# Turned scores in a top-k attention kernel: products of k and q in place of transpositions

## The chip, the cores and the metric

The kernel runs on one core of one Trainium2 chip. A core has a matrix engine (TensorE, PE in the profile; its weight loads are PEld), a vector engine (VectorE, DVE), a scalar engine (ScalarE, ACT), GpSimd (POOL) and a queue engine for transfers (SyncE, SP). The metric is the device time of one execution in microseconds. The kernel before takes 929.28 us, the median of three runs (928.62 to 929.35).

## The reference

Eight batches of eight heads, 576 positions, 64 numbers a head, all fp32. First attention that keeps the 32 highest scores of each row, then a mixture-of-depths layer on the result.

```python
scores = scale * np.matmul(q, k.transpose(0, 1, 3, 2))
kth = np.partition(scores, -top_k, axis=-1)[..., -top_k:-top_k + 1]
scores = np.where(scores >= kth, scores, -1000000000.0)
attn = np.exp(scores - np.max(scores, axis=-1, keepdims=True))
attn = attn / (np.sum(attn, axis=-1, keepdims=True) + 1e-09)
x = np.matmul(attn, v)                    # then (B, H, S, D) -> (B, S, H*D)

scores = np.einsum('bsd,d->bs', x, w_gate)
for b in range(B):                        # the 128 positions with the highest gate
    top_idx = np.argpartition(-scores[b], capacity)[:capacity]
    xe = x[b, top_idx]
    ye = np.maximum(xe @ w1, 0.0) @ w2
    g = 1.0 / (1.0 + np.exp(-scores[b, top_idx]))
    out[b, top_idx] = x[b, top_idx] + g[:, None] * ye
```

The expert's hidden width is 1024.

## The kernel before

**Units.** The work is cut into units of two heads by up to 128 rows of q. A batch has four row tiles of 128 rows with four units each (t = 0 to 3, "whole units") and a last row tile of 64 rows (t = J = 4) with two units, in which four heads are stacked two by two on the 128 partitions ("stacked units"): 18 units a batch, 144 in all.

**The pipeline.** A loop over n (lines 758 to 862) works on several units at once, and every engine executes its instructions in the order written there:

- unit n+1: `multiply` makes the scores, rows of q on the partitions, as k and q products in PSUM (`ps`); `keep` copies them to SBUF as `sc` on ScalarE.
- unit n: `find_bound` on VectorE takes the highest 8 of each of 8 pieces of a row and narrows them to the 24th highest of these candidates.
- unit n-1: two sign passes (`part`) on ScalarE count and mark what lies above that bound, and GpSimd multiplies scores and signs into `y`.
- unit n-2: `find_kth` on VectorE finds the 32nd highest from `y`.
- unit n-3: `mask` makes `less` (bf16), larger than zero where a score is below the 32nd: ScalarE for the first head, GpSimd for the second.
- unit n-4: the scores are needed turned, with keys on the partitions, for the product with v. `turn_last` and `turn` transpose `sc` on TensorE, nine tiles of 128x128, and behind each transposition a second matmul adds `less` times `out_of_reach` (a diagonal of -2^90) into the same PSUM, so that masked scores vanish in the exponential. ScalarE takes exponentials from PSUM (`last`, then `pT` for each head) and `values` multiplies them by v on TensorE.

In one turn of the loop TensorE's order is: turning of unit n-4, scores of unit n+1, values of unit n-4, then a step of the mixture of the batch before (expert products `h_ps`, `y_ps`) or of the load of the next batch, as `mix_at` and `load_at` (lines 728 and 737) set them. ScalarE's is: exponentials of n-4, copies put off by `late` (flushed at line 786), the mask of n-3, the score copies of n+1, the sign passes of n-1, the copies of the values.

**The buffers.** kT and qT of a batch hold k and q with the 64 numbers of a head on the partitions, heads of even number on partitions 0 to 63 and of odd number on 64 to 127; there are two such pairs, taken in turn by the batches. `load_kq` fetches rows, transposes them on TensorE, and copies them in. Keys 0 to 511 stand in kT at R to S (R = 64, S = 576); the last 64 stand at 0 to R and again behind. PSUM's `ps` is one buffer: the turning of the tail (`tr_last`) uses 128 columns of it that the scores of unit n+1 leave free. The score products of two heads stand on the two 64-row halves of the array. `general`, at the end, is a path for data that the fast one can't treat; the run does not enter it.

Of the kernel before, what the change touches and what calls it, by code (L numbers as in the profile page):

```python
# [11 lines left out]
FP32 = mybir.dt.float32  # L12
# [18 lines left out]
J = 4  # L31
# [14 lines left out]
def kernel(  # L46
# [12 lines left out]
    P = nc.NUM_PARTITIONS  # L59
    B, H, S, D = q.shape  # L60
# [4 lines left out]
    JP = J * P  # L65
    R = S - JP
# [22 lines left out]
    ps_tr = ctx.enter_context(tc.tile_pool(name="ps_tr", bufs=2, space=PS))  # L89
# [4 lines left out]
    ident = const.tile([P, P], FP32, name="ident")  # L94
# [24 lines left out]
    out_of_reach = const.tile([P, P], BF16, name="out_of_reach")  # L119
# [25 lines left out]
    vbufs = []  # L145
# [13 lines left out]
    def load_weights():  # L159
# [6 lines left out]
    pe, dve, act, pool, sp = (  # L166
        InOrder(tc, e)
        for e in (nc.tensor, nc.vector, nc.scalar, nc.gpsimd, nc.sync)
    )
# [13 lines left out]
        flush()  # L183


    def room_for_qkv(b):

        kT = kqpool.tile([P, NHP, R + S], FP32, name="kT")
        qT = kqpool.tile([P, NHP, S], FP32, name="qT")
        return kT, qT, vbufs[b % 2]

    def load_kq(kb, qb, kT, qT, issue=None):

        last = [ldpool.tile([R, H, D], FP32, name=f"last{i}", bufs=1) for i in range(2)]

        def fetch_last(w, dma):
            src = (kb, qb)[w]
            dma.dma_start(
                out=last[w], in_=src[:, JP:S, :].rearrange("h p d -> p h d")
            )

        def fetch(i, dma=sp):
            hp, src = i // 2, (kb, qb)[i % 2]
            rows = ldpool.tile([P, J, 2, D], FP32, name="rows")
            for hh in range(2):  # L210
                dma.dma_start(
                    out=rows[:, :, hh, :],
                    in_=src[2 * hp + hh, 0:JP, :].rearrange("(p j) d -> p j d", j=J),
                )
            return rows

        issue = issue or sp
        fetch_last(0, sp)
        fetch_last(1, issue)
        fetched = [fetch(0), fetch(1, issue), fetch(2)]  # L220
        yield
        tr = ps_misc.tile([P, 512], FP32, name="tr", tag="misc")
        for i in range(2 * NHP):
            w, hp = divmod(i, NHP)
            pe.transpose(
                tr[:, i * R : (i + 1) * R],
                last[w][:, 2 * hp : 2 * hp + 2, :].rearrange("p h d -> p (h d)"),
                ident[0:R, 0:R],
            )

        def keep_last(tails=tr.rearrange("p (w c r) -> p w c r", w=2, c=NHP)):
            act.copy(out=kT[:, :, 0:R], in_=tails[:, 0, :, :])
            act.copy(out=kT[:, :, S : S + R], in_=tails[:, 0, :, :])
            act.mul(out=qT[:, :, JP:S], in_=tails[:, 1, :, :], mul=SMALLER)

        late.append(keep_last)
        yield
        for i in range(2 * NHP):
            tr = ps_misc.tile([P, 512], FP32, name="tr", tag="misc")
            for c in range(J):  # L240
                pe.transpose(
                    tr[:, c * P : (c + 1) * P],
                    fetched[i][:, c, :, :].rearrange("p h d -> p (h d)"),
                    ident,
                )

            def keep_rows(i=i, tr=tr):
                if i % 2 == 0:
                    act.copy(out=kT[:, i // 2, R:S], in_=tr)
                else:  # L250
                    act.mul(out=qT[:, i // 2, 0:JP], in_=tr, mul=SMALLER)

            late.append(keep_rows)
            if i + 3 < 2 * NHP:
                fetched.append(fetch(i + 3))
            yield

    def load_v(vb, vs):
        vt, vpair = vs
        v_rows = vb[:, JP:S, :].rearrange("h p d -> p h d")  # L260
        for hh in range(2):
            sp.dma_start(
                out=vpair[hh * R : (hh + 1) * R, :, hh, 0:D], in_=v_rows[:, hh::2, :]
            )
        for h in range(H):
            sp.dma_start(
                out=vt[:, h, :, 0:D],
                in_=vb[h, 0:JP, :].rearrange("(p j) d -> p j d", j=J),
            )
# [5 lines left out]
    def heads_of(t, g):  # L275

        if t == J:
            return [[(4 * g + i, 0), (4 * g + 2 + i, R)] for i in range(2)]
        return [[(2 * g + i, 0)] for i in range(2)]
# [107 lines left out]
                )  # L391
        return less

    def turn_some(tr, z, less):

        pe.transpose(tr, z, ident)
        if less is not None:
            pe.matmul(
                tr, less, out_of_reach, start=False, stop=True, skip_group_check=True
            )  # L400

    def turn(i, z, less=None):

        tr = ps_tr.tile([P, 512], FP32, name="ptr")
        for c in range(J):
            at = slice(c * P + i * R, (c + 1) * P + i * R)
            turn_some(
                tr[:, c * P : (c + 1) * P],
                z[:, i, at],
                None if less is None else less[:, i, at],  # L410
            )
        return tr

    def turn_last(z, ps, less=None):

        tr = ps[:, 1, 1, 512 - P : 512]
        last = [  # L420
            a and a.rearrange("p i s -> p (i s)")[:, JP : JP + P] for a in (z, less)
        ]
        turn_some(tr, *last)
        return tr

    def values(t, g, pT, last, av, vs):
# [296 lines left out]
    units = [(b, t, g) for b in range(B) for t in range(NT) for g in range(groups(t))]  # L723
# [19 lines left out]
                break  # L743
            mix_steps.setdefault(n, []).append(b)
    mixtures = {}
    qkv = {0: room_for_qkv(0)}
    first_load = load_kq(k[0], q[0], *qkv[0][0:2], issue=act)
    next(first_load)
    next(first_load)
    flush()  # L750
# [7 lines left out]
    for n in range(-1, N + 6):  # L758
# [11 lines left out]
        if is_unit(n - 4) or is_unit(n + 1):  # L770
            ps = room_for_scores()
        if is_unit(n - 4):
            sc, less = scs.pop(n - 4), masks.pop(n - 4)
            tr_last = turn_last(sc, ps, less)
            trs = [turn(i, sc, less) for i in range(2)]
            pT = ptpool.tile([P, 2, J, P], FP32, name="pT")
            last = ptpool.tile([P, P], FP32, name="last")
            act.activation(last, tr_last, AF.Exp, scale=scale)
            for i in range(2):
                act.activation(  # L780
                    pT[:, i, :, :],
                    trs[i].rearrange("p (c i) -> p c i", c=J),
                    AF.Exp,
                    scale=scale,
                )
# [55 lines left out]
        if gating is not None:  # L841
            b, t = gating
# [11 lines left out]
        if n in load_steps:  # L854
            b, begin = load_steps[n]
            if begin:
                qkv[b] = room_for_qkv(b)
                loading = load_kq(k[b], q[b], *qkv[b][0:2])
            next(loading)
        b, i = divmod(n, per_batch)  # L860
        if i == v_at and 0 <= b < B - 1:
            load_v(v[b + 1], qkv[b + 1][2])

    for b in (B - 2, B - 1):
        for _ in mixtures[b]:
# [65 lines left out]
    def general(b, row0):  # L931
        def of(a):
            return a[bass.ds(b, 1)].rearrange("o a s d -> (o a) s d")

        kT, qT, vs = room_for_qkv(0)
        for _ in load_kq(of(k), of(q), kT, qT):
            flush()
        load_v(of(v), vs)
        x = xpool.tile([P, NT, HD], FP32, name="x")
        gate = xpool.tile([P, NT], FP32, name="gate")  # L940
        for t in range(NT):
            xs = xpool.tile([P, H, DE], FP32, name="xs")
            for g in range(groups(t)):
                ps = room_for_scores()
                multiply(t, g, kT, qT, ps)
                p = general_weights(keep(ps))
                ps = room_for_scores()
                av = ps_av.tile([P, 512], FP32, name="av")
                pT = ptpool.tile([P, 2, J, P], FP32, name="pT")
                last = ptpool.tile([P, P], FP32, name="last")  # L950
                for i in range(2):
                    nc.scalar.copy(
                        out=pT[:, i, :, :],
                        in_=turn(i, p).rearrange("p (c i) -> p c i", c=J),
                    )
                nc.scalar.copy(out=last, in_=turn_last(p, ps))
                values(t, g, pT, last, av, vs)
                keep_values(t, g, av, xs)
            rows = R if t == J else P
            den = stats.tile([P, H], FP32, name="den")  # L960
            divide(rows, xs, x[0:rows, t, :], den[0:rows, :])
            dot_tile(t, x, gate)
        store(out[bass.ds(b, 1)].rearrange("o s n -> (o s) n"), x)
        rank = stats.tile([P, NT], FP32, name="rank")
        for _ in mixture(row0, gate, rank, exact=True):
            flush_both()
# [40 lines left out]
```

## Time and profile before

| | |
|---|---|
| median of three runs | 929.28 us |
| the profiled execution, own time | 923.33 us |
| its span, first to last instruction | 921.5 us |
| mean granted TensorE clock | 0.975 |
| busy share of the span: TensorE, VectorE, ScalarE, GpSimd | 88%, 90%, 84%, 79% |
| start of the first turning | 37.4 us |
| mean time of a batch (18 units), batches 1 to 6 | 104.8 us |

The page gives busy time, groups of instructions by form with their mean duration, idle time and what ended it; the timeline gives instructions by start time, runs of equal ones merged into one line with their count. TensorE's instructions are pipelined, so a mean duration is longer than the distance between two starts. Nearly all instructions are recorded at line 42, that of the helper that issues them; so groups are told by their tiles (out<-in).

### The profile page before, as it was taken

How to read it: one execution, taken by the hardware profiler on the slowest of the kernel's cores; microseconds unless marked ns; L12 is line 12 of the kernel's file. 1: busy time of each engine (PE TensorE's matmuls, PEld its weight loads, DVE VectorE, ACT ScalarE, POOL GpSimd, SP SyncE). 2: the span in 40 equal slices, each digit the busy share in tenths (PEclk: the TensorE clock that was granted, in tenths of full speed). 3: DMA queues.
4: the chain of work that ended last, by engine and by line, in shares of the span. 5: the costliest groups of instructions: out<-in, count | busy, mean ns of one | idle time of the engine just before them, and what ended most of it. 6: DMA issues, size and time to landing. Idle time of an engine off the chain costs nothing.

```text
span 921.5 us, 28585 instructions
## 1 busy us (share of the span) xinstructions
PE 808.6 (88%) x9839; PEld 617.3 (67%) x9839; DVE 832.5 (90%) x4966; ACT 772.5 (84%) x1883; POOL 732.4 (79%) x800
## 2 busy tenths in 40 slices
PE   5699889788999899998999889998999889987935
PEld 3477666566877678766777668766787667765723
DVE  4799999999999999999999999999999999998140
ACT  3699998898998899989998999989998898987310
POOL 2589998888988898888988898889888898888210
PEclk9999999999999999999999999999999999998968
DMA  5952005112140313221140313222150211000021
GB/s 102 265 116 59 14 2 124 30 36 47 65 89 7 57 34 101 53 48 47 66 89 2 59 36 99 55 48 48 47 107 2 37 53 26 3 14 13 1 74 15
DMA packets 122200, 50.40 MB, mean 55 GB/s; under 512 B 116416, under 2 KB 116416, under 8 KB 121024
## 3 DMA queue, kind: packets, MB, share of 16 engines
q1 hardware_dynamic: 118672, 43.91, 20.3%
q0 software_dynamic: 1792, 4.20, 2.6%
q8 instruction: 80, 1.31, 0.6%
q14 instruction: 72, 0.59, 0.3%
q10 hardware_dynamic: 1584, 0.39, 0.2%
HBM read 36.93 MB, written 11.55 MB: 53 GB/s over the span
## 4 chain that ended last, share of the span: by engine, by line
DVE 35%; PE 28%; ACT 20%; POOL 6%; DMA 5%; issue 4%; SPq 0%; POOLq 0%; ACTq 0%
DVE cand L42 18%; DVE next L42 8%; ACT sides L42 7%; PE ptr L42 7%; PE ps L42 6%; ACT sc L42 5%; PE av L42 5%; PE h_ps L42 5%; DVE best L42 5%; PE y_ps L42 5%; ACT pT L42 3%; POOL y L42 2%; POOL less L42 2%; DMA row_dram<-gate 2%; DVE prod L42 2%
## 5 line engine op out<-in xcount | busy, mean ns | idle before, releaser
L42 POOL TENSOR_TENSOR y<-sc,sides 128x576 f32<-128x576 f32 x288 | 367.1, 1306 | 101.7 <-ACT sides L42 101.3
L42 DVE MAX8 cand<-sc 128x8 f32<-128x72 f32 x2304 | 331.5, 217 | 16.0 <-ACT sc L42 16.0
L42 POOL TENSOR_SCALAR less<-sc,next 128x576 bf16<-128x576 f32 x144 | 256.7, 1783 | 26.9 <-DVE next L42 17.9
L42 ACT ACTIVATE sides<-sc,seen 128x576 bf16<-128x576 f32 x288 | 221.0, 768 | 4.9
L42 PE MATMUL ptr<-ident,sc 128*128 128x128 f32 x1152 | 218.2, 283 | 0.0
L42 DVE MAX8 next<-y 128x8 f32<-128x584 f32 x288 | 204.4, 751 | 6.2 <-POOL y L42 6.2
L42 PE MATMUL ptr<-out_of_reach,less 128*128 128x128 bf16 x1152 | 209.5, 222 | 0.0
L42 PE MATMUL ps<-kT,qT 64*128 64x288 f32 (+1 forms) x1280 | 187.2, 449 | 18.2 <-ACT last L42 13.1
L42 ACT ACTIVATE pT<-ptr 128x512 f32<-128x512 f32 x288 | 163.2, 597 | 32.3 <-PE ptr L42 26.7
L42 PEld LDWEIGHTS av<-v,pT 128*64 128x64 f32 x4608 | 147.2, 138 | 57.5 <-ACT pT L42 30.7
L42 ACT COPY sc<-ps 128x576 f32<-128x576 f32 x288 | 170.7, 654 | 11.9 <-PE ps L42 10.8
L42 PEld LDWEIGHTS ptr<-ident,sc 128*128 128x128 f32 x1152 | 164.9, 143 | 14.4
L42 PEld LDWEIGHTS <-less 128*128 128x128 bf16 x1296 | 134.5, 105 | 59.2 <-POOL less L42 50.2
L42 PE MATMUL av<-v,pT 128*64 128x65 f32 x4608 | 167.5, 225 | 0.3 <-ACT pT L42 0.2
L42 DVE MAX8 best<-cand 128x8 f32<-128x64 f32 x864 | 148.8, 213 | 0.0
L42 PEld LDWEIGHTS ps<-kT,qT 64*128 64x128 f32 (+1 forms) x1280 | 100.2, 184 | 65.0 <-ACT last L42 29.0
L42 ACT ACTIVATE less<-sc,next 128x576 bf16<-128x576 f32 x144 | 113.2, 786 | 10.2 <-DVE next L42 9.8
L42 DVE MATCH_REPLACE8 cand<-best,cand 128x64 f32<-128x64 f32 x576 | 116.1, 209 | 0.0
L42 PE MATMUL ps<-out_of_reach,less 128*128 128x128 bf16 x144 | 32.2, 224 | 42.0 <-POOL less L42 42.0
L42 PE MATMUL av<-vpair,last 128*128 128x130 f32 (+1 forms) x320 | 69.0, 316 | 0.0
L42 PE MATMUL h_ps<-xeT,w 128*128 128x128 f32 x512 | 63.8, 282 | 3.8 <-ACT xeT L42 2.0
L42 PEld LDWEIGHTS h_ps<-xeT,w 128*128 128x128 f32 x512 | 60.6, 196 | 6.0 <-ACT xeT L42 2.7
(80 smaller groups left out, 842.5 us busy)
## 6 DMA issues: line engine op xcount, KB each, us to landing
rows<-in_k_dram SPq DMA_DIRECT2D x64, 128.0 KB, 3.0
v<-in_v_dram SPq DMA_DIRECT2D x64, 128.0 KB, 3.5
out_dram<-x SPq DMA_DIRECT2D x8, 1024.0 KB, 4.6
rows<-in_q_dram SPq DMA_DIRECT2D x62, 128.0 KB, 3.2
w<-in_moe_w_dram SPq DMA_DIRECT2D x2, 2048.0 KB, 13.3
gate_row<-row_dram SPq DMA_DIRECT2D x7, 288.0 KB, 4.3
last<-in_k_dram SPq DMA_DIRECT2D x8, 128.0 KB, 4.5
vpair<-in_v_dram SPq DMA_DIRECT2D x16, 64.0 KB, 3.4
```

The source lines that it names most:

```text
L42: return lambda *a, **kw: self._tc.keep_in_program_order(fn(*a, **kw))
```

## The change

The turned scores are no longer transposed from `sc` but made by a second set of products, with kT as the weights and qT streaming, for the two heads on the two 64-row halves of the array: nine tiles as before, and the mask is added behind as before. The products of the tail and of the first 128 keys stand ahead of the first mask product, then the products of the other keys, then eight mask products. Since kT and qT of a batch are now read until its last unit is turned (five turns of the loop longer), the room for the next batch's is taken only when the first copy into it is made. `turn` and `turn_last` lose their mask and serve only `general`.

```diff
+    qkv = {}
     def room_for_qkv(b):
...
-        return kT, qT, vbufs[b % 2]
-    def load_kq(kb, qb, kT, qT, issue=None):
+        qkv[b] = kT, qT, vbufs[b % 2]
+        return qkv[b]
+    def load_kq(kb, qb, room, issue=None):
+        kept = []
...
         def keep_last(tails=tr.rearrange("p (w c r) -> p w c r", w=2, c=NHP)):
+            kept.extend(room()[0:2])
+            kT, qT = kept
             act.copy(out=kT[:, :, 0:R], in_=tails[:, 0, :, :])
...
             def keep_rows(i=i, tr=tr):
+                kT, qT = kept
...
+    def multiply_turned(t, g, kT, qT, ps, less):
+        n = R if t == J else P
+        rows = heads_of(t, g)
+        tr_last = ps[:, 1, 1, 512 - P : 512]
+        trs = [ps_tr.tile([P, 512], FP32, name="ptr") for _ in range(2)]
+        for i in range(2):
+            d = slice(i * D, (i + 1) * D)
+            for h, r in rows[i]:
+                pe.matmul(
+                    tr_last[i * R : (i + 1) * R, r : r + n],
+                    kT[d, h // 2, 0:R],
+                    qT[d, h // 2, t * P : t * P + n],
+                    start=(r == 0),
+                    stop=False,
+                    skip_group_check=True,
+                )
+        for c in range(J):
+            for e in range(len(rows[0])):
+                for i in range(2):
+                    d = slice(i * D, (i + 1) * D)
+                    h, r = rows[i][e]
+                    pe.matmul(
+                        trs[i][:, c * P + r : c * P + r + n],
+                        kT[d, h // 2, R + c * P : R + (c + 1) * P],
+                        qT[d, h // 2, t * P : t * P + n],
+                        start=(c == 0 and r == 0),
+                        stop=False,
+                        skip_group_check=True,
+                    )
+            if c == 0:
+                put_out(tr_last, less.rearrange("p i s -> p (i s)")[:, JP : JP + P])
+        for i in range(2):
+            for c in range(J):
+                at = c * P + i * R
+                put_out(trs[i][:, c * P : (c + 1) * P], less[:, i, at : at + P])
+        return tr_last, trs
+    def put_out(tr, less):
+        pe.matmul(tr, less, out_of_reach, start=False, stop=True, skip_group_check=True)
...
         if is_unit(n - 4):
-            sc, less = scs.pop(n - 4), masks.pop(n - 4)
-            tr_last = turn_last(sc, ps, less)
-            trs = [turn(i, sc, less) for i in range(2)]
+            b, t, g = units[n - 4]
+            scs.pop(n - 4)
+            tr_last, trs = multiply_turned(t, g, *qkv[b][0:2], ps, masks.pop(n - 4))
...
             if begin:
-                qkv[b] = room_for_qkv(b)
-                loading = load_kq(k[b], q[b], *qkv[b][0:2])
+                loading = load_kq(k[b], q[b], lambda b=b: room_for_qkv(b))
             next(loading)
...
-            load_v(v[b + 1], qkv[b + 1][2])
+            load_v(v[b + 1], vbufs[(b + 1) % 2])
```

More of the change, by code (lines that the diff above doesn't have):

```diff
@@ L392, in mask @@
         return less
[L394 to L402, printed above, removed]
+    def multiply_turned(t, g, kT, qT, ps, less):
[34 more added lines that the diff above has]
+        return tr_last, trs
@@ L404, in turn @@
+    def put_out(tr, less):
+        pe.matmul(tr, less, out_of_reach, start=False, stop=True, skip_group_check=True)
+    def turn(i, z):
         tr = ps_tr.tile([P, 512], FP32, name="ptr")
         for c in range(J):
[L406 to L411, printed above, removed]
+            at = c * P + i * R
+            pe.transpose(tr[:, c * P : (c + 1) * P], z[:, i, at : at + P], ident)
@@ L412, in turn, with turn_last @@
         return tr
-    def turn_last(z, ps, less=None):
+    def turn_last(z, ps):
         tr = ps[:, 1, 1, 512 - P : 512]
[L420 to L423, printed above, removed]
+        pe.transpose(tr, z.rearrange("p i s -> p (i s)")[:, JP : JP + P], ident)
         return tr
@@ L745 @@
     mixtures = {}
-    qkv = {0: room_for_qkv(0)}
-    first_load = load_kq(k[0], q[0], *qkv[0][0:2], issue=act)
+    room_for_qkv(0)
+    first_load = load_kq(k[0], q[0], lambda: qkv[0], issue=act)
     next(first_load)
@@ L935, in general @@
         kT, qT, vs = room_for_qkv(0)
-        for _ in load_kq(of(k), of(q), kT, qT):
+        for _ in load_kq(of(k), of(q), lambda: qkv[0]):
             flush()
```

## The prediction

> **What bounds the kernel now.** I read the page's engine shares first, then busy time by stretches, then the groups by form, the timeline of TensorE, and last the waits.
>
> ```profile
> PE 808.6 (88%) x9839; PEld 617.3 (67%) x9839; DVE 832.5 (90%) x4966; ACT 772.5 (84%) x1883; POOL 732.4 (79%) x800
> ```
>
> ```profile
> 353.00:397.50 44.50, 44.13 (x527) 33.80 (x526) 44.09 (x272) 41.21 (x100) 38.60 (x43) 1.00 0.31 77
> 397.50:449.60 52.10, 46.11 (x622) 36.01 (x621) 51.89 (x306) 48.51 (x121) 45.73 (x50) 1.00 0.21 42
> ```
>
> The columns are stretch, length, then busy us of PE, PEld, DVE, ACT, POOL, the clock, and DMA. VectorE is busy 99% of both stretches; TensorE is busy 99% of the first (a batch's middle, where the expert products of the batch before are mixed in) and 89% of the second. So two engines sit at their limits at once: no gain on TensorE can shorten the middle by more than VectorE's 1%, and any lengthening of TensorE shows at once in the first stretch.
>
> The forms of TensorE's work:
>
> ```profile
> L42 PE MATMUL ptr<-ident,sc 128*128 128x128 f32 x1152 | 218.2, 283 | 0.0
> L42 PE MATMUL ptr<-out_of_reach,less 128*128 128x128 bf16 x1152 | 209.5, 222 | 0.0
> L42 PE MATMUL ps<-kT,qT 64*128 64x288 f32 x1024 | 164.4, 441 | 17.2 <-ACT last L42 12.3 <-ACT qT L42 2.7 <-ACT sc L42 1.3
> ```
>
> The counts tell most. 144 units with 8 transpositions each make 1152, one instruction each. But 128 whole units with 4 score products make 512, and the row has 1024: an fp32 product costs two instructions, a transposition one. Means overlap, so spacing has to come from start times:
>
> ```profile
> 387.24 1.24 PE L42 MATMUL ps<-kT,qT 64*128 64x288 f32 x8
> 388.41 1.16 PE L42 MATMUL av<-v,pT 128*64 128x65 f32 x32
> 389.50 0.49 PE L42 MATMUL av<-vpair,last 128*128 128x130 f32 x2
> 389.82 1.88 PE L42 MATMUL y_ps<-w,hT 128*128 128x512 f32 x4
> 391.54 0.27 PE L42 MATMUL ps<-ident,sc 128*128 128x128 f32 x1
> ```
>
> This unit began its turning at 385.62: turning 1.62 us, scores 1.17, attention values 1.09 and 0.32, expert products 1.72, and the next unit's turning starts without a gap. It is TensorE-bound. The spacings and the price of changing the array's tiling:
>
> ```profile
> 450.99 0.28 PE L42 MATMUL ptr<-ident,sc 128*128 128x128 f32 x1
> 451.11 0.22 PE L42 MATMUL ptr<-out_of_reach,less 128*128 128x128 bf16 x1
> 451.26 1.00 PE L42 MATMUL ps<-kT,qT 64*128 64x288 f32 x6
> ```
>
> ```profile
> 404.24 0.51 PE L42 MATMUL ps<-kT,qT 64*128 64x288 f32 x2 [0.32 <-ACT last L42]
> ```
>
> ```profile
> 404.59 0.65 PE L42 MATMUL ps<-kT,qT 64*128 64x288 f32 x4
> ```
>
> ```profile
> 405.07 0.41 PE L42 MATMUL ps<-kT,qT 64*128 64x288 f32 x2
> ```
>
> ```profile
> 446.85 2.94 PE L42 MATMUL h_ps<-xeT,w 128*128 128x128 f32 x24
> ```
>
> A transposition takes 0.115 to the next start, a mask product 0.057: a pair 0.171. Score instructions start two at a time on the two 64-row halves, 0.24 apart (404.59, 404.83, 405.07) for 288 columns. Full fp32 instructions of 128 columns run every 0.112 (2.94 for 24, the tail of one off). From a mask product (full array) to the first score product (halves) the distance is 0.15 instead of 0.057: 0.093 for the change of tiling. Then the first pair lasts 0.35 instead of 0.24: 0.105 of weight load that nothing covers.
>
> ```profile
> PE ps L42 <- POOL less L42: 42.0, 39, 3.6
> PEld av L42 <- ACT pT L42: 30.7, 79, 0.5
> ACT pT L42 <- PE ptr L42: 26.7, 63, 1.0
> ```
>
> Outside the dense stretch TensorE waits for the mask from GpSimd, 42 us in 39 of 144 units.
>
> **The change, part by part.** Removed per unit: 9 transpositions. Kept: 9 mask products. Added in a whole unit (128 rows; 128 units): 10 fp32 products, that is 20 instructions. 16 of them load 64x128 weights (128 keys of one head), 4 load 64x64 (the last 64 keys); each streams 128 queries. If the halves run together as the score products do, that is 10 slots. No row has this form; the nearest is the 0.112 of the expert products (same 128 columns, weights as wide), and two 64-row weight loads start together in the score products. 10 x 0.112 = 1.12, masks 9 x 0.057 = 0.51: 1.63 against 9 x 0.171 = 1.54 before. Bounds: 1.07 by scaling the score slot (0.24 x 128/288 x 10), 2.24 if the halves take turns.
>
> Added tilings: the old block keeps the full array throughout. The new one enters 64x64 tiles, goes to 64x128, to the full array for the first mask, back to 64x128, and again to the full array for eight masks: five changes more. Each costs 0.093 by the row above. The weights behind each: 0.105 into 128 fp32 columns (twice), 0.053 into 64 columns (estimated as half), 0.025 into a bf16 mask (twice; bounded by 0 and 0.105, the low end because bf16 loads of 128 columns have the shorter mean, 105 ns against 143). Sum 5 x 0.093 + 0.313 = 0.78; the ends are 0 (all hidden) and 0.99 (0.198 each). I take 0.78, from the rows of exactly such changes. The block: 1.63 + 0.78 = 2.41, so 0.87 more.
>
> The last-row-tile units (16, two a batch) stack two heads in 64-column products: 40 instructions, 20 slots. The 16 with 128-column weights are bounded below by 0.056 (half the columns) and above by 0.112; I take 0.112 as the load is as wide. 4 tail slots at 0.062 (32 attention-value instructions in 1.16, two at a time). 1.79 + 0.25 + 0.51 + 0.78 = 3.33: 1.79 more.
>
> The Trainium skill, "TensorEngine Tiling (Array Packing)", section Tiling Modes, says that changing the tiling mode, not just the tile, drains the engine; that speaks against interleaving masks with half-array products, and the 0.093 above agrees with it. It names no lost weight load; with drains alone the block would be 1.63 + 0.47 = 2.10 and the same sum as below would give some 980 instead.
>
> Where this lands. By the starts of the tail's transposition, one for each unit, batches 1 to 6 take 104.8 us on average. Of the 18 units up to 441.89, the ten from 338.40 to 397.47 (with expert products, or loads' transpositions between them) run with TensorE back to back, 59.07 us. Their nine whole and one stacked unit get 9 x 0.87 + 1.79 = 9.6 us, all on the path. The other eight (397.47 to 441.89, 44.4 us) hold TensorE waits: the turning block has mean 2.13 against its 1.54, about 10 us a batch. The added 7.9 there falls mostly into these waits, yet ScalarE's exponentials come later: the first head's masks were half done in the middle of the old block, now they end 0.23 before its close, 2.2 us after its start instead of 0.86. ScalarE covers this by its two sign passes (about 2.0 us after the score copies free PSUM), so some 0.2 to 0.3 a unit shows, and the queue behind it is the mask, then the score copies that free PSUM for the next block. I take 1 of the 0 to 2.5 us. 10.6 a batch over seven batches is 74; batch 0 (96.9 us, no expert products) 3. Start and end stay. Together 77: the profiled execution's 923.3 (span 921.5) becomes 1000, and the median 929.3 becomes 1006; I say 1004, a little under because a few of the ten units have short waits.
>
> The new wait: the first mask still waits for GpSimd, now with 4 products done and 6 products and 8 masks behind it, 1.5 us against the old 1.43. So where the mask is late nothing is won.
>
> Other edits, at nothing: kT and qT get their room in the tail copies instead of at the fetch. Those copies stand in ScalarE's order after the exponentials of the very unit that last reads the old kT, so they wait for nothing new, and the batch that needs them is 15 units off; if the cover went, one unit (5.8 us) a batch, seven times 5.8 at most, and only if it reached the scores. SP's fetches keep their places, and so do the value loads. Score buffers come free one step earlier; ScalarE's copies waited only 1.0 us for that. VectorE, ScalarE and GpSimd issue the same.
>
> **The rivals.** (a) The changes of tiling are hidden, the weights loaded ahead: the block is 1.63 and 2.55, the dense stretch gains 9 x 0.09 + 1.01 = 1.8 a batch, 13 in all: 942. For it: full-array weight loads are covered (0.112 a slot). Against: the 0.15 and 0.35 above.
> (b) The halves take turns: 1.12 more in a whole unit, 2.04 in a stacked one. TensorE's work in a batch is 18 x (1.54 + 1.17 + 1.09 + 0.32) = 74, loads 4, expert products 64 x 0.112 + 16 x 0.43 = 14, together 92 of 104.8; it becomes 92 + 17.5 + 22 = 131.5; seven batches of +28 and some 16 in the first: about 1145. Against: the score products' pairs.
> (c) Faster: the wait for the mask sets the pace, and behind it less is left: with free changes 6 x 0.112 + 0.51 = 1.18 instead of 1.43, in 39 units, 10 us: 919. It decides only if the two changes behind the first mask cost under 0.25 together (the rows say 0.32) and the dense stretch does not grow, while even free changes leave 1.63 over 1.54.
>
> **How the numbers follow.** Main case 0.66, its own range 970 to 1045; (a) 0.21, 930 to 970; (b) 0.07; (c) 0.04; no change 0.02. 0.2% is about what a measurement of this kernel can tell from none. Slower 0.94, same 0.02, faster 0.04. The range 945 to 1045 leaves out (b), (c), and the low part of (a).
>
> **What would show it.** About 3200 product instructions in place of 1296 transpositions. From the first tail product to the first score product about 2.4 us (3.3 stacked) in units without a wait; a unit with four y_ps instructions 6.8 instead of 5.92; a batch about 115 instead of 104.8. VectorE keeps 832 us busy but falls to about 84%, the wait of PE for POOL less shrinks well below 42. Wrong if products start singly, if first pairs behind a mask are no later than others, or if the dense stretch has slack that the busy time hides.

## The result, and the profile after

The changed kernel takes 991.18 us (median of 4 runs, 989.9 to 995.07) against 928.95 for the kernel before: 1.068 times as long, 95% interval 1.065 to 1.071. Its profiled execution took 991.56 us with a span of 989.7; the span of before was 921.5, so the two traces differ by 68 us, of which the medians show 62: the profiled execution of before (923.3 us) was faster than its timed runs here and beside the experiments, which, but for one slow run of 1403.9, took 924.2 to 935.5.

The first line of the page, then the same two stretches of a batch as in the prediction, moved to where they now lie:

```profile
PE 916.8 (93%) x11743; PEld 681.5 (69%) x11743; DVE 867.5 (88%) x4966; ACT 772.1 (78%) x1883; POOL 735.8 (74%) x800
```

```profile
371.90:422.40 50.50, 50.50 (x612) 36.20 (x608) 46.37 (x270) 40.55 (x99) 38.33 (x43) 1.00 0.27 64
422.40:469.10 46.70, 44.00 (x635) 33.37 (x634) 44.90 (x251) 40.89 (x98) 39.98 (x43) 1.00 0.23 47
```

TensorE is now busy all through the dense stretch (50.50 of 50.50 us), while VectorE, 99% before, has fallen to 92% there. TensorE alone sets the pace. One dense unit with four expert products, from TensorE's timeline:

```profile
407.91 0.44 PE L42 MATMUL ps<-qT,kT 64*64 64x128 f32 x4
408.28 0.49 PE L42 MATMUL ptr<-qT,kT 64*128 64x128 f32 x4
408.70 0.23 PE L42 MATMUL ps<-out_of_reach,less 128*128 128x128 bf16 x1
408.86 0.94 PE L42 MATMUL ptr<-qT,kT 64*128 64x128 f32 x12
409.73 0.62 PE L42 MATMUL ptr<-out_of_reach,less 128*128 128x128 bf16 x8
410.28 1.24 PE L42 MATMUL ps<-kT,qT 64*128 64x288 f32 x8
411.45 1.15 PE L42 MATMUL av<-v,pT 128*64 128x65 f32 x32
412.53 0.49 PE L42 MATMUL av<-vpair,last 128*128 128x130 f32 x2
412.86 1.88 PE L42 MATMUL y_ps<-w,hT 128*128 128x512 f32 x4
```

Turning goes from 407.91 to 410.28, 2.37 us instead of 1.62, and everything behind it is as long as before. The next unit begins at 414.67: 6.76 us for the unit instead of 5.92. The difference is 0.84, not 0.75, because the change of tiling in front of the block lies in the y_ps products' distance to it. Within the block the tail's second pair of products starts 0.16 after the first, the products' second pair 0.21 after theirs, later pairs 0.11 apart, and the masks 0.056.

The rows of waits:

```profile
ACT pT L42 <- PE ptr L42: 91.7, 143, 1.8
PEld av L42 <- ACT pT L42: 56.4, 141, 0.7
PE ps L42 <- POOL less L42: 14.8, 15, 2.2
```

ScalarE now waits for the turned scores in 143 of 144 units, 92 us instead of 27; TensorE's wait for GpSimd's mask has fallen from 42 us to 15.

By the start of each unit's block, the 68 us lie here: batch 0 takes 104.7 us instead of 96.9, batch 1 as long as before (106.9 and 107.0), batches 2 to 6 take 114.3 on average instead of 104.4 (+49.8 together), the last +10.6. Before the first block and behind the last nothing has moved (37.5 and 52.3 us in both). Of the +9.9 in such a batch, 7.6 are in the ten dense units (59.07 to 66.63) and 2.4 in the eight others (45.3 to 47.7).

The granted clock has a part in the last number. In the trace of before there are spells of 3.41 us in which TensorE is granted half its clock: one each in batches 1, 2, 4 and 6, none in batches 3 and 5. The changed kernel has none in batches 0 to 6. What a spell costs can be read from two units of before, the same one of batch 2 and of batch 3: both wait 1.84 us for GpSimd's mask, but only in the first does a spell follow (the third line; columns as in the prediction, the clock behind POOL):

```profile
302.65:310.76 8.11, 6.27 (x74) 4.15 (x75) 8.04 (x50) 5.89 (x15) 6.72 (x8) 0.79 0.63 99
407.44:414.11 6.67, 4.75 (x73) 3.52 (x74) 6.63 (x41) 5.56 (x14) 6.67 (x8) 1.00 0.76 119
305.56:308.97 3.41, 3.41 (x26) 1.73 (x24) 3.41 (x15) 2.34 (x4) 3.41 (x4) 0.50 0.84 148
```

That is 1.44 us more. Before's two batches at full clock take 103.5 us, 44.4 of them in the eight units; against these the changed kernel lost 7.6 in the dense ten and 3.3 in the eight, 10.8 a batch.

### The profile page after: what moved, and what is told of

It is laid out like the page before. It is cut to its first block, busy times and chain, and to the rows that moved or that the text cites. A ratio compares the mean times of both kernels' runs of the same rounds, so it can differ in the third digit from the quotient of the medians.

```text
span 989.7 us, 32393 instructions
## 1 busy us (share of the span) xinstructions
PE 916.8 (93%) x11743; PEld 681.5 (69%) x11743; DVE 867.5 (88%) x4966; ACT 772.1 (78%) x1883; POOL 735.8 (74%) x800
## 4 chain that ended last, share of the span: by engine, by line
PE 48%; DVE 33%; ACT 11%; DMA 4%; POOL 2%; issue 2%; SPq 0%; POOLq 0%; ACTq 0%
DVE cand L42 16%; PE ptr L42 16%; PE ps L42 12%; PE av L42 8%; DVE next L42 7%; PE h_ps L42 6%; PE y_ps L42 5%; DVE best L42 4%; ACT sc L42 3%; ACT pT L42 3%; DVE pick L42 2%; ACT less L42 2%; DMA row_dram<-gate 1%; DVE junk L42 1%; PE tr L42 1%
## 5 line engine op out<-in xcount | busy, mean ns | idle before, releaser
L42 POOL TENSOR_TENSOR y<-sc,sides 128x576 f32<-128x576 f32 x288 | 371.3, 1322 | 183.4 <-ACT sides L42 183.2
L42 ACT ACTIVATE pT<-ptr 128x512 f32<-128x512 f32 x288 | 156.3, 594 | 91.7 <-PE ptr L42 91.7
L42 PE MATMUL ptr<-qT,kT 64*128 64x128 f32 (+1 forms) x2560 | 220.0, 295 | 0.0
L42 PEld LDWEIGHTS ptr<-qT,kT 64*128 64x128 f32 x2560 | 166.3, 187 | 32.8 <-issue 22.1
L42 PE MATMUL ps<-kT,qT 64*128 64x288 f32 (+1 forms) x1280 | 185.1, 440 | 4.1 <-ACT qT L42 2.7
L42 PEld LDWEIGHTS <-less 128*128 128x128 bf16 x1296 | 79.1, 98 | 49.3 <-POOL less L42 17.8
L42 PE MATMUL ptr<-out_of_reach,less 128*128 128x128 bf16 x1152 | 90.1, 222 | 0.0
L42 PE MATMUL ps<-qT,kT 64*64 64x128 f32 (+1 forms) x640 | 63.3, 283 | 13.4 <-ACT sc L42 10.6
L42 ACT ACTIVATE last<-ps 128x128 f32<-128x128 f32 x144 | 39.6, 275 | 44.9 <-PE ps L42 44.7
```

The lines of the kernel that those rows point to most:

```text
L42: return lambda *a, **kw: self._tc.keep_in_program_order(fn(*a, **kw))
```

## Experiments

The theory: TensorE's own time in the dense stretch sets the loss, through the fp32 products' two instructions and five more changes of tiling. The first rival: lateness, the exponentials coming later on ScalarE. In the table, "behind the mask" is TensorE's work from the instruction that waits for GpSimd's mask to the end of the block (without the change of tiling to the scores), worked out from the spacings of the timelines; "wait" is the sum of TensorE's and its weight loads' waits for that mask (POOL less), which mostly run at the same time, so that it measures more than was lost; ten and eight are the dense and the other units of a batch (batches 2 to 6); "spells" are the spells of half clock in these five batches, and "eight, full clock" is the mean of the eight in those batches that have none. Times of before on the same chips: 928.7 to 929.9.

| kernel | whole block, no wait | behind the mask | wait | ten | eight | spells | eight, full clock | median |
|---|---|---|---|---|---|---|---|---|
| before | 1.63 | 1.43 | 92 | 59.1 | 45.3 | 3 | 44.4 | 929 |
| changed | 2.37 | 1.49 | 33 | 66.6 | 47.7 | 0 | 47.7 | 991 |
| changed, products first | 2.07 | 0.50 | 21 | 63.6 | 44.8 | 0 | 44.8 | 947 |
| changed, masks first | 1.96 | 1.96 | 111 | 62.7 | 49.8 | 5 | none | 986 |
| before, changes of tiling added | 2.13 | 1.93 | 78 | 63.0 | 48.0 | 7 | 45.9 | 961 |
| before, masks last | 1.58 | 0.51 | 35 | 59.5 | 43.8 | 0 | 43.8 | 917 |
| before, tail's mask in the middle | 1.58 | 0.97 | 53 | 59.6 | 44.7 | 1 | 44.5 | 923 |
| before, first head's masks ahead | | | 27 | 61.1 | 43.2 | 0 | 43.2 | 918 |
| before, tail in another bank | | | 46 | 60.0 | 43.5 | 0 | 43.5 | 917 |

In "changes of tiling added" the eight take 45.9 us with no spell, 47.3 with one and 48.8 to 48.9 with two, which is the same price of 1.4 to 1.5 us. In the kernels of this table the spells in these batches follow waits of TensorE of 1.7 to 2.3 us for GpSimd's mask; but like waits also pass without one, as above, and what sets a spell off isn't shown.

### The price of a change of tiling

```diff
     tr_last = turn_last(sc, ps, less)
-    trs = [turn(i, sc, less) for i in range(2)]
+    half_array(ps)
+    trs = [turn(0, sc, less)]
+    half_array(ps)
+    trs.append(turn(1, sc, less))
+def half_array(ps):
+    pe.matmul(ps[:, 0, 0, 300:302], out_of_reach[0:R, :], out_of_reach[0:R, 0:2])
```

> The kernel before, with a product of 64 rows and 2 columns put ahead of each head's transpositions: four changes of tiling a unit and no other work to speak of. Theory (changes cost 0.093 to 0.104 each plus the uncovered weight load behind them): the turning block grows from 1.63 to about 2.3 us, ten dense units by 7, a batch by 8 to 9, the kernel to 975 to 990. Rival (the changes are cheap where weights can be fetched ahead, and the fp32 products are the price): under 940.

960.7 us, 1.032 times before (1.027 to 1.038). The timeline of one unit:

```profile
383.92 0.22 PE L42 MATMUL ps<-out_of_reach,less 128*128 128x128 bf16 x1
384.07 0.17 PE L42 MATMUL ps<-out_of_reach 64*128 64x2 bf16 x1
```

The half-array product starts 0.15 after the mask instead of 0.056, so about 0.095 for the change; the transposition behind it starts 0.10 later, and the first mask after that 0.05 late. An excursion costs 0.25, two of them 0.50 (block 2.13, unit with four y_ps 6.43). My block of 2.3 meant about 0.34: the weights of a transposition leave only 0.05 uncovered, not 0.105. Changes of tiling alone, with the transpositions kept, so cost half of what the changed kernel lost, which is against the rival that the products are the price. The half also holds at full clock: the one batch without a spell takes 109.0 us, against 103.5 in before and 114.3 in the changed kernel. The expectation for the time was too high, for that reason and because some of the ten units have slack (+3.9 for 10 x 0.50).

### Fewer changes: all products first

```diff
-            if c == 0:
-                put_out(tr_last, less.rearrange("p i s -> p (i s)")[:, JP : JP + P])
+        put_out(tr_last, less.rearrange("p i s -> p (i s)")[:, JP : JP + P])
         for i in range(2):
```

> The changed kernel with all products ahead of all nine masks: two changes of tiling fewer, the tail's exponential later. Theory: 0.30 us less a whole unit (0.093 + 0.104 of changes, 0.10 of weights), the block 2.07, a batch 4 less, 960 to 967. Rival (lateness on ScalarE): the first exponential comes 1 us later into the block, no gain, 985 to 995.

946.6 us, 1.019 times before (1.013 to 1.024). The block is 2.07 and the dense ten 3.0 shorter, exactly as the prices of two changes and their weights have it. But the kernel gained 44.6 us, not 28: the other eight units gained 2.9 (47.7 to 44.8), nearly as much as the dense ones. Something else was in it. Nor did the first exponential come 1 us later: in units without a wait it starts 1.95 us into the block, and 2.25 in the changed kernel, so this run doesn't test lateness.

### Still fewer: the masks first

On the kernel with all products first, the nine masks go ahead of the products for the tail and for keys 0 to 511, which add to them:

```diff
         trs = [ps_tr.tile([P, 512], FP32, name="ptr") for _ in range(2)]
+        put_out(
+            tr_last,
+            less.rearrange("p i s -> p (i s)")[:, JP : JP + P],
+            start=True,
+        )
+        for i in range(2):
+            for c in range(J):
+                at = c * P + i * R
+                put_out(
+                    trs[i][:, c * P : (c + 1) * P],
+                    less[:, i, at : at + P],
+                    start=(c == 0),
+                )
...
-                    start=(r == 0),
-                    stop=False,
+                    start=False,
+                    stop=True,
...
-        put_out(tr_last, less.rearrange("p i s -> p (i s)")[:, JP : JP + P])
-        for i in range(2):
-            for c in range(J):
-                at = c * P + i * R
-                put_out(trs[i][:, c * P : (c + 1) * P], less[:, i, at : at + P])
```

> The changed kernel with the nine masks ahead of the products, so that one change to 64x64, one to 64x128 and none before the scores is left. Theory: 0.63 us less a unit than the changed kernel, 0.2 more than before in a whole unit and 1.0 in a stacked one, so 2.8 a batch: 940 to 955; the wait for the mask from GpSimd returns to about 40 us. Rival (lateness, both exponentials at the block's end): over 965.

985.6 us, 1.058 times before (1.052 to 1.065): the number of the rival, 39 us behind the kernel with the products first, with a shorter block (1.96 against 2.07) and a shorter dense stretch (62.7 against 63.6). The eight other units take 49.8 instead of 44.8, and the rows of waits say why:

```profile
PEld L42 <- POOL less L42: 67.5, 62, 4.0
PE ps L42 <- POOL less L42: 43.4, 32, 3.2
```

With the products first the same rows hold 11.7 and 9.3 us. The two kernels do the same work on every engine. What differs above all is what stands behind the mask: 1.96 us or 0.50. Neither of my theories had this as its own term. Two other things are in the 5.0 us of the eight: each batch of the masks-first kernel has one spell of half clock and the other none, which at 1.44 leaves 3.6; and the first head's exponential starts 0.20 us later in a unit without a wait, whose share isn't separated.

### Lateness without other work: the transpositions first, the masks last

`turn_bare` does the four transpositions of `turn` without the masks; `put_out` is that of the change.

```diff
-    tr_last = turn_last(sc, ps, less)
-    trs = [turn(i, sc, less) for i in range(2)]
+    tr_last = turn_last(sc, ps)
+    trs = [turn_bare(i, sc) for i in range(2)]
+    put_out(tr_last, less.rearrange("p i s -> p (i s)")[:, JP : JP + P])
+    for i in range(2):
+        for c in range(J):
+            at = c * P + i * R
+            put_out(trs[i][:, c * P : (c + 1) * P], less[:, i, at : at + P])
```

> The kernel before, its nine transpositions first and the nine mask products after them: the same work and tilings on TensorE, but both heads' exponentials come late, as in the changed kernel. Theory (the loss is TensorE's own time in the dense stretch: 0.84 us a whole unit, 1.64 a stacked one): no loss, 922 to 932. Rival (the loss is the lateness of the first head's exponentials on ScalarE, 1.3 us in the changed kernel and 0.5 here): a third of the 62 us, about 950.

916.9 us, 0.988 of before (0.985 to 0.991): no loss, as the theory has it, but neither of the two had a gain. Counted from the block's start, the first head's exponential comes up to 0.41 us later in the dense units; over all, it is later in 74 of 144 units and earlier in 24. Lateness of this size costs no more than the 0.4 us by which the dense ten grow (59.1 to 59.5), and the rival falls in the size that it was given; the 1.2 us of the changed kernel aren't tested by themselves. The wait for GpSimd's mask goes from 92 to 35 us, and the eight fall from 45.3 to 43.8. This version is faster than both kernels.

Most of the gain goes with the clock, which neither of the two considered. Batches 2 to 6 of masks last take 103.4 us each and have no spell of half clock; those of before take 103.5 without a spell and 104.8 to 105.1 with one. So nearly all that masks last wins in these batches, 4.7 us, it wins where before has a spell; three spells at 1.44 us are 4.3. Outside the traces it fits that the mean granted clock of the ten runs of masks last is 0.970 to 0.983, that of the thirteen of before beside them 0.954 to 0.974. That the shorter wait is what keeps the clock up is likely and not shown.

### The tail's mask in the middle

```diff
     tr_last = turn_last(sc, ps)
-    trs = [turn_bare(i, sc) for i in range(2)]
+    trs = [turn_bare(0, sc)]
     put_out(tr_last, less.rearrange("p i s -> p (i s)")[:, JP : JP + P])
+    trs.append(turn_bare(1, sc))
```

> The kernel before with its masks last (916.9), but the tail's mask already after the first five transpositions, so that the tail's exponential is done when the scores are to start. Theory (late exponential of the tail holds up the score products, 69 us of waits there): these waits go, 908 to 915. Rival (what stands behind the mask decides: 0.97 us again instead of 0.51): 919 to 926.

923.2 us, 0.994 of before (0.991 to 0.997): the rival's number. One mask product moved forward by four transpositions puts 0.97 us behind the mask, the wait rises from 35 to 53 us, and half of the gain is gone. With 1.43, 0.97 and 0.51 us behind the mask the kernel takes 929, 923 and 917 us. The batches at full clock aren't in that order, though: 103.5, 104.1 and 103.4 us. So this row of times doesn't show that the work behind the mask is paid for directly.

### The first head's masks before GpSimd's

The first head's four masks need only ScalarE's part of `less`. The tail's exponential moves behind the first head's.

```diff
-            tr_last = turn_last(sc, ps, less)
-            trs = [turn(i, sc, less) for i in range(2)]
+            trs = [turn_bare(0, sc)]
+            for c in range(J):
+                put_out(trs[0][:, c * P : (c + 1) * P], less[:, 0, c * P : (c + 1) * P])
+            tr_last = turn_last(sc, ps)
+            trs.append(turn_bare(1, sc))
+            put_out(tr_last, less.rearrange("p i s -> p (i s)")[:, JP : JP + P])
+            for c in range(J):
+                at = c * P + R
+                put_out(trs[1][:, c * P : (c + 1) * P], less[:, 1, at : at + P])
...
-            act.activation(last, tr_last, AF.Exp, scale=scale)
...
+                if i == 0:
+                    act.activation(last, tr_last, AF.Exp, scale=scale)
```

> The kernel before in a new order: the first head's four transpositions and its four masks (ScalarE's mask alone), then the tail's and the second head's five transpositions, then the five masks that need GpSimd's; the exponentials in the same order. Same work on TensorE. Theory (what stands behind GpSimd's mask decides the light units, TensorE's time the dense ones): 0.28 us stand behind it instead of 1.43, and the first head's exponential is early; the dense ten stay at 59 to 59.6, the light eight fall to 43 to 44: 908 to 916, not behind the 917 of the masks at the end. Rival (the gain of the masks at the end came from something else, such as the tail's transposition being ahead): 925 to 930.

917.8 us, 0.989 of before (0.984 to 0.994), a little over the range of the theory. The wait for the mask falls to 27.5 us and the eight to 43.2, but the dense ten rise to 61.1: the tail's exponential now comes behind the first head's, and the score products wait for it.

```profile
PEld ps L42 <- ACT last L42: 91.8, 139, 2.0
PE ps L42 <- ACT last L42: 59.1, 78, 1.8
```

These rows were 29.0 and 13.1 us in before. A unit with four y_ps takes 6.10 instead of 5.92. What was won at the mask was lost there.

### The tail in another bank

The turned tail takes free columns of the values' `av` instead of the scores' `ps`; its exponential is now the last of the three.

```diff
-            tr_last = turn_last(sc, ps, less)
-            trs = [turn(i, sc, less) for i in range(2)]
+            trs = [turn_bare(i, sc) for i in range(2)]
+            for i in range(2):
+                for c in range(J):
+                    at = c * P + i * R
+                    put_out(trs[i][:, c * P : (c + 1) * P], less[:, i, at : at + P])
+            av = ps_av.tile([P, 512], FP32, name="av")
+            tr_last = av[:, 512 - P : 512]
+            turn_some(tr_last, *[
+                a.rearrange("p i s -> p (i s)")[:, JP : JP + P] for a in (sc, less)
+            ])
...
-            act.activation(last, tr_last, AF.Exp, scale=scale)
...
+            act.activation(last, tr_last, AF.Exp, scale=scale)
```

> The kernel before with eight transpositions first, then the masks of both heads, the tail's transposition and mask at the end and in the bank of the values (av) instead of that of the scores (ps); exponentials of the heads first. So the block no longer waits for the score copies to free ps, and the score products no longer for the tail's exponential. Theory (in the kernel with masks last these two waits, 69 and 52 us, set the light units; TensorE the dense ones): dense ten 59 to 59.5, light eight 43 or less, 905 to 915. Rival (the values' copies on ScalarE, after the sign passes, now hold the block up, or VectorE is the floor): no gain over 917, up to 935.

916.9 us, 0.987 of before (0.984 to 0.990): the rival's number, level with the masks last. The score products no longer wait for the tail's exponential, and the rows of its waits at ps for the score copies hold 2.1 and 1.3 us. In their place the values wait, for the tail's exponential, which now comes last, and for the copies `xs` out of `av`:

```profile
PEld av L42 <- ACT last L42: 56.3, 135, 1.2
PEld av L42 <- ACT xs L42: 55.5, 72, 1.8
```

TensorE's own instructions wait 42.8 us for `xs` besides. The wait for GpSimd's mask is 46 us. Three different orders end at 917 to 918 us, with batches 2 to 6 of 103.4, 104.5 and 103.6 us on average, and before at full clock takes 103.5. Which limit they share isn't settled. VectorE is near it: in the middle of these traces (240 to 760 us) its idle time, and what its short instructions pick, sums and prod take above their usual 0.27, 0.15 and 0.67 us, come together to 14 to 19 of 520 us (17 in before).

### One turn of the loop later

The turning, the values and their copies work on unit n-5 in place of n-4.

```diff
-    scpool = ctx.enter_context(tc.tile_pool(name="sc", bufs=5))
+    scpool = ctx.enter_context(tc.tile_pool(name="sc", bufs=6))
...
-    stats = ctx.enter_context(tc.tile_pool(name="stats", bufs=6))
+    stats = ctx.enter_context(tc.tile_pool(name="stats", bufs=5))
...
-        less = wkpool.tile([P, 2, S], BF16, name="less")
+        less = wkpool.tile([P, 2, S], BF16, name="less", bufs=3)
...
-    mix_at = (5, 6, 9, 10, 13, 14, 15, 16, 19, 21, 23, 25, 27, 28, 29, 30, 31)
+    mix_at = (6, 7, 9, 10, 13, 14, 15, 16, 19, 21, 23, 25, 27, 28, 29, 30, 31)
...
-        if is_unit(n - 4):
-            sc, less = scs.pop(n - 4), masks.pop(n - 4)
+        if is_unit(n - 5):
+            sc, less = scs.pop(n - 5), masks.pop(n - 5)
```

> The kernel before with the turning, exponentials and values one turn of the loop later (unit n-5; one more buffer for scores and one for masks), so that the mask is ready long before it is needed. Theory (grouping the masks won 12 us because less work stood behind GpSimd's mask): the wait for it falls from 92 us to under 15, the light eight units of a batch fall from 45.6 to about 44, the dense ten stay at 59, and the kernel takes 912 to 922. Rival (that gain came from the shorter block on TensorE, 0.05 us a unit, or the exponentials' order): 927 to 931.

943.0 us (median of three runs), 1.016 times before (1.008 to 1.022). The edit also takes one buffer from the small tiles of `stats`; no wait of VectorE on it shows in the trace. The wait for GpSimd's mask did go (50.2 to 1.1 us of TensorE's weight loads), and the time got worse. The row that replaced it:

```profile
PE place_ps L42 <- DVE pick L42: 39.4, 12, 6.7
```

TensorE now reaches the placing of the chosen rows before VectorE has chosen them, up to 6.7 us at a time (6.9 us in all before). So I moved that step:

```diff
-    load_at = (2, 4, 6, 8, 13, 14, 16, 17, 18)
+    load_at = (2, 4, 6, 8, 13, 14, 15, 17, 18)
...
-    mix_at = (6, 7, 9, 10, 13, 14, 15, 16, 19, 21, 23, 25, 27, 28, 29, 30, 31)
+    mix_at = (6, 7, 9, 10, 13, 14, 16, 17, 19, 21, 23, 25, 27, 28, 29, 30, 31)
```

> The kernel with the turning one turn later (943.6), with the step that places the chosen rows, and the gather behind it, one unit later too (the load beside it one earlier), since TensorE had come to wait 39 us there for VectorE's choice. Theory (that wait, not the later turning, cost the time; and without GpSimd's wait the light units are shorter): 912 to 922, the light eight about 44. Rival (the longer pipeline itself costs, or the wait moves on to VectorE's other results): 930 or over.

932.9 us (the ten runs lie between 922.9 and 943.1), level with before (0.996 to 1.005): the rival again. The wait moved on to the score copies:

```profile
PEld ps L42 <- ACT sc L42: 63.0, 63, 5.7
```

22.3 us in before. TensorE runs a turn ahead of the engines that it needs and waits for them elsewhere. Of batches 2 to 6 four take 108.4 to 108.5 us and one 104.2; the four hold a wait of some 5.4 us for the score copies and behind it 6.8 us at half clock, the one neither. Why these waits come is open.

### The halves one after the other

```diff
-        for c in range(J):
-            for e in range(len(rows[0])):
-                for i in range(2):
+        for i in range(2):
+            for c in range(J):
+                for e in range(len(rows[0])):
```

(on the kernel with all products first)

> The kernel with all products ahead of the masks (946.6), but the products for keys 0 to 511 of the first head all before those of the second. Theory (the halves only run together when their instructions alternate): 8 slots of 0.111 more in a whole unit, 16 of 0.105 in a stacked one, blocks of 2.96 and 4.6 us, a batch 17 more, about 1075. Rival (the engine brings them together whatever their order): 947.

1041.5 us, 1.122 times before (1.116 to 1.128). Sixteen instructions in a row, from TensorE's timeline:

```profile
423.03 0.44 PE L42 MATMUL ps<-qT,kT 64*64 64x128 f32 x4
423.39 1.71 PE L42 MATMUL ptr<-qT,kT 64*128 64x128 f32 x16
425.04 0.23 PE L42 MATMUL ps<-out_of_reach,less 128*128 128x128 bf16 x1
```

They take 1.65 us to the first mask, 1.10 when they alternate. Fully apart they would need 0.89 more, and 0.55 is what is seen: by the starts, three instructions of the second head run beside those of the first, and the rest alone. So both were partly wrong: the engine reaches ahead for the other half, but only over a few instructions.

### The later room

> The kernel before with only the room for kT and qT taken at the first copy into it. Theory: nothing, 927 to 932. Rival (the later room delays the loads of the next batch): a few us more, 933 or over.

928.7 us, 0.999 of before (0.996 to 1.002): the kernel before with only this edit. It costs nothing.

## Why the prediction was right, point by point

**The block.** The mechanism was right. Predicted 0.87 us more in a whole unit, measured 0.84; 1.79 more in a stacked one, measured 1.64 (3.18 instead of 1.63 up to the scores, and the change in front). Pairs of 128-column products do start 0.111 apart, as the expert products' row had it. Changes of tiling cost 0.09 to 0.10 each; the uncovered weights 0.095 for 128 fp32 columns, 0.047 for 64 and 0.01 for a bf16 mask, against 0.105, 0.053 and 0.025. Drains alone, the other reading that the prediction gave, would have made 980 us, and they are out: the first pairs, 0.21 instead of 0.11 apart, show the weights as well.

**The dense stretch.** 9.6 us a batch was predicted, 7.6 measured. The mis-sized term is "all on the path": three of the four units with y_ps got the full 0.83 to 0.84, but the fourth got 0.63 (6.13 to 6.76), those with h_ps 0.54 and 0.53 (7.19 to 7.73, 6.30 to 6.83), and the stacked one 0.79 instead of 1.79 (7.74 to 8.53). So the ten did not run back to back, as the prediction read them: in before's timeline the blocks of these units hold waits of 0.20, 0.30, 0.30 and 0.85 us, for the tail's exponential and, in the stacked one, for GpSimd's mask too. The text had left 2 us in all for this; it was 2 a batch.

**The other eight units.** 1 us a batch was predicted from a range of 0 to 2.5; it was 2.4 on average, but 3.3, over the range, against the batches of before at full clock, and the window that the prediction took its 44.4 from is one of these. The change also ended the spells of half clock, which the prediction did not have, and that hid 0.9. So it was luck that a batch came out so near: 10.6 predicted, 10.8 measured at full clock, by two errors of about 2 us with opposite signs. The mechanism is the one named: ScalarE waits for the turned scores, then its mask and the score copies come late, and the next block waits for ps. The experiments add what the prediction touched only in its paragraph on the new wait: 1.49 us behind the mask against 1.43, as worked out there (1.5), so the work behind the mask did not shrink, while all products ahead of the masks took 45 us off the changed kernel, with two changes of tiling fewer.

**How many batches.** The sum took seven dense stretches and 3 us for batch 0. Batch 1 has no expert products under its ten units and lost nothing; so six stretches paid, not seven. Batch 0 lost 7.8 and not 3, in units with loads and without expert products; that the later exponentials on ScalarE draw it out is argued only. Together 68 us were measured between the traces, 77 predicted.

**VectorE.** Predicted: 832 us busy, 84%. The page says 867.5, 88%, with as many instructions. These two rows, before and after, show why:

```profile
L42 DVE TENSOR_SCALAR pick<-slot,ranks 64x128 bf16<-64x128 bf16 x8 | 3.3, 409 | 0.3
```

```profile
L42 DVE TENSOR_SCALAR pick<-slot,ranks 64x128 bf16<-64x128 bf16 x8 | 15.2, 1902 | 0.3
```

The instruction and its count are the same, so the added time isn't work of its own. All six records of 2.2 to 3.6 us in the changed kernel overlap GpSimd's multiplications into `y`, and the one of each kernel with no GpSimd instruction beside it takes 0.25 us. That GpSimd is what holds them isn't tested. Before has some of this too (its eight take 0.25 to 0.72 us), so not all of its 832 us was work. The prediction's sentence that nothing on TensorE can shorten the middle by more than VectorE's 1% spoke of the dense stretch, and there it held in every order of masks and transpositions that was tried. For the whole kernel it would be too strong: the masks last won 1.2% (0.9 to 1.5) with the same work.

**The rivals.** (a) fell with the 0.16 and 0.21 gaps; (b) with the pairs, and the halves apart gave its price, 0.55 us a unit rather than 1.12 (its sum also has 28 us a batch where 131.5 less 104.8 is 26.7, about 1132 rather than 1145). (c), the wait for the mask, was priced at 10 us and given 4 in 100 as a way for this change to win. Moving the masks did win 12 us, in the traces mostly where before has spells of half clock, but the change as written left as much behind the mask as before. The later room cost nothing, as said.

## What to carry to other kernels

Count instructions, not operations: an fp32 product is two instructions here and a transposition one, so running the two halves together only made up for the doubling, and each change of tiling put 0.09 us or more and an uncovered weight load on top. When an engine waits in order for something late, ask what stands behind that wait: two orders of the same products and masks lay 39 us apart, and in the kernel before moving the masks behind the transpositions won 12, with no less work. Before you put such a gain down to the wait itself, compare stretches at the same granted clock: at full clock the batches of those last two kernels took 103.5 and 103.4 us. And taking a wait away by a longer pipeline only pays if the engine does not run into the next one.

## What was not expected of the hardware

- A change between the full array and 64-row halves costs 0.09 to 0.10 us in the timelines read here without a wait, even for a product of 2 columns (0.095).
- Of two halves' instructions given one after the other, three ran together in the stretch shown; alternating, all do.
- Records of short VectorE instructions grew up to fivefold (409 to 1902 ns on average) where the kernel as a whole got slower: a mean that grows at an unchanged count tells of a hold-up that no idle time shows.
- A spell of half the granted clock lasts 3.41 us and cost 1.44 us in a unit that is otherwise the same (8.11 against 6.67). In the kernels of the table such spells came after waits of about 2 us, but not after each; with the halves apart, batches 2 to 6 have them with no wait ahead.
